# Windowed attention and expert routing on one Trainium2 core: the filling transposes get a PSUM bank of their own, the routing constants become one product, scales are spread in bfloat16

## The chip, the cores and the metric

One NeuronCore of a Trainium2 chip runs the whole kernel; the other cores are idle. The metric is the device time of one execution in microseconds (us). TensorE (PE) multiplies matrices out of SBUF into PSUM, VectorE (DVE) and ScalarE (ACT) work element by element, GpSimd (POOL) does so too and issues the gathers and scatters, SyncE (SP) issues most DMAs.

## The reference, cut to what matters

Four batches of eight heads, 768 positions and 64 dimensions go through a windowed attention; its output is 3072 tokens of 512 values, which a mixture of eight experts works on. Every expert takes exactly 384 tokens, and which ones is settled greedily over all 3072 x 8 scores:

```
logits = x @ w_gate
order = np.argsort(-logits.flatten())
for idx in order:
    tok, e = idx // E, idx % E
    if assigned[tok] >= 0 or counts[e] >= cap: continue     # cap = 384
    assigned[tok] = e; counts[e] += 1
...
for e in range(E):
    h = np.maximum(x[assigned == e] @ w1[e], 0.0)           # 384 x 512 x 1024
    out[assigned == e] = h @ w2[e]                          # 384 x 1024 x 512
```

## The kernel before, in words

**Attention** (lines 55 to 266) runs over 24 tiles of 128 tokens as a software pipeline: scores (L104), softmax on DVE and ACT (L112 to L116), transposes (L123, L192), the product with the values (L138), logits (L203, L213). SP loads each tile's keys, values and queries into one of five buffers (L92) when the buffer is free. POOL and ACT build a two-part float16 copy of each token row (L172 to L174), and SP stores it to memory (`xs`, L182).

**Constants** (L917 to L963) are made while the attention runs: one table is loaded into `cc`, and POOL casts its pieces (L935, L948), after which DVE copies some of them into a PSUM tile `R` (L952 to L958). `constants` is a generator that is advanced once per attention tile; all nine casts and `pairs` stand in one step of it.

**Routing** (`phase`, L461) finds one expert's 384 tokens at a time. For each of the first seven experts it makes four rounds of a search: DVE builds two masks (L384), PE counts into a histogram `ps` (L396), DVE clips it (`hs`, L510), PE forms running counts (L522, L524), DVE counts the cells at or over 384 (`rc`, L529), PE spreads the result over all partitions (L533 with a base, L534 with the counts), and DVE takes the maximum (`nm`, L537). After the fourth round the expert's number is known (`ei`, L544; the weight loads of that expert wait for it), and slots follow: a scan (L569), the offset of each partition (L579, L580), masks (L594 to L601), a product that sorts the token numbers (L631, L636), the numbers themselves (`ids`, L642), and three gathers of token rows by POOL (L647). For the first expert POOL first clears a row of the three targets (L627), after a small read `seen` that waits for all stores of `xs` (L625).

**Experts**: each expert's weights come as float32 tiles of 128 x 1024 (L736, 16 buffers). ACT takes their absolute sums (L749), PE and DVE make a power of two of them (L752, L754, L758, `pow2`), PE spreads it over the partitions (L761, with a float32 row of ones), ACT copies it (L766) and scales and rounds the weights (L788, L790), POOL makes the low parts (L799, L816). For the first expert the rows are transposed on PE (`turn`, L674) and copied by ACT and DVE (L677, L679). `gemm` does 96 products of 128 x 384 (L862) and 72 of 128 x 512 (L877) per expert, three passes each for high and low parts. The loads of the first expert's second matrix are held back by a one-element ACT copy (L731).

**What sets the order.** `Lines` (L406) is a planner. Every line of work is a generator that names an engine, an estimated cost and a ready time; `run` takes the line that can start first and emits its instructions, so these estimates set each engine's program order. While the first expert is being routed nothing else is there for PE, so `fill` (L454) puts dummy transposes of a 128 x 128 identity matrix into the planned gaps. Before, they write into columns 384 to 448 of the PSUM tile `D`:

```
n = int((t - self.clk[PE] - 0.2) / 0.11)
for _ in range(n):
    g.nc.tensor.transpose(g.D[:, 384:448].bitcast(F16), g.ident16, g.ident16)
```

`D` is one bank, and it also holds the histogram, the running counts, the offsets, `quads` and a row of ones, each of which DVE or ACT reads or writes.

Of the kernel before, what the change touches and what calls it, by code (L numbers as in the profile page):

```python
# [11 lines left out]
F32 = mybir.dt.float32  # L12
F16 = mybir.dt.float16
BF16 = mybir.dt.bfloat16
# [5 lines left out]
P = 128  # L20
# [4 lines left out]
NT = N // P  # L25
# [376 lines left out]
LATE, SEM = 0.25, 0.1  # L402
# [3 lines left out]
class Lines:  # L406
# [47 lines left out]
    def fill(self, t):  # L454
        g = self.g
        n = int((t - self.clk[PE] - 0.2) / 0.11)
        for _ in range(n):
            g.nc.tensor.transpose(g.D[:, 384:448].bitcast(F16), g.ident16, g.ident16)  # L458


def phase(g, k, out):  # L461
# [12 lines left out]
    if k < E - 1:  # L474
# [11 lines left out]
        for r in range(4):  # L486
            if k or r:
# [5 lines left out]
                for a, b in zip(cuts, cuts[1:]):  # L493
# [8 lines left out]
                    p = yield PE, 0.2 + 0.015 * (b - a), max(e + SEM, p)  # L502
# [24 lines left out]
            rc = t([64, 1], F16, "rc")  # L527
# [7 lines left out]
            e = yield DVE, 0.55, p + LATE  # L535
# [20 lines left out]
    e = yield DVE, 1.6, e  # L556
# [12 lines left out]
    v.tensor_tensor_scan(R.sc, g.one48, gq.rearrange("p a n -> p (a n)"), 0.0, op0=ALU.mult, op1=ALU.add)  # L569
# [3 lines left out]
    v.tensor_scalar(g16, gq, 1.0 / 16, None, op0=ALU.mult)  # L573
# [3 lines left out]
    p = yield PE, 0.3, e + SEM  # L577
# [39 lines left out]
def tokens(g, k, out, lo, hi, e):  # L617
# [10 lines left out]
    p = yield PE, 0.45, e + SEM, soon  # L628
# [85 lines left out]
def loads(g, k, st):  # L714
# [25 lines left out]
def weights(g, k, st, n):  # L740
# [20 lines left out]
    nc.tensor.matmul(g.D[:, 106:108], g.one_row, pr.rearrange("p a b -> p (a b)"), start=True, stop=True)  # L761
# [155 lines left out]
def constants(g, consts):  # L917
# [9 lines left out]
    for t, x in ((g.ones, 1.0), (g.one_row, 1.0), (g.esum, 28.0)):  # L927
        nc.gpsimd.memset(t, x)
    for _ in range(5):
        yield  # L930
    g.e8 = c["e8"]

    def cast(n, dt, rows=P):
        t = g.fixed.tile([rows, c[n].shape[1]], dt, name="c_" + n)
        nc.gpsimd.tensor_copy(t, c[n][:rows])  # L935
        return t

    g.upper = cast("upper", BF16)
    g.tri2, g.eye2 = (cast(n, F16).rearrange("p (a m) -> p a m", a=2) for n in ("tri2", "eye2"))
    g.blk, g.base = cast("blk", F16, 64), cast("base", BF16, 2)  # L940
# [7 lines left out]
    nc.gpsimd.tensor_copy(pairs, c["io"][:, 0:E * 8].unsqueeze(2).to_broadcast([P, E * 8, 2]))  # L948
# [4 lines left out]
    nc.vector.memset(R.z0, 0.0)  # L953
    nc.vector.tensor_copy(R.idc.bitcast(I32), idc.bitcast(I32))
    g.one48 = g.D[:, 204:252]
    nc.vector.memset(g.one48, 1.0)
    nc.vector.memset(g.one48[:, NT:NT + 1], 0.0)
    nc.vector.tensor_copy(R.e8, g.e8)  # L958
    g.quads = g.D[:, 448:480].bitcast(BF16).rearrange("p (n t) -> p n t", t=4)
    quads = g.fixed.tile([P, 16, 4], BF16, name="quads")  # L960
    nc.gpsimd.tensor_copy(quads, c["six"].unsqueeze(2).to_broadcast([P, 16, 4]))
    g.quads0 = quads
    yield  # L963
# [3 lines left out]
def attention_moe(ctx: ExitStack, tc: tile.TileContext, kv, w_gate, w1, w2, consts, out):  # L967
# [14 lines left out]
    g.ones = g.fixed.tile([P, P], BF16, name="ones")  # L982
    g.one_row = g.fixed.tile([1, P], F32, name="one_row")
# [6 lines left out]
    with tc.manual_schedule():  # L990
        with (tc.tile_pool(name="abuf", bufs=1) as g.abuf, tc.tile_pool(name="kvbuf", bufs=1) as g.kvbuf,
# [9 lines left out]
            g.lines, g.cold, g.open = Lines(g), INF, False  # L1001
# [13 lines left out]
        g.wbuf = ctx.enter_context(tc.tile_pool(name="wbuf", bufs=1))  # L1015
        g.lines.run()
# [23 lines left out]
CONST_COLS = [("io", P), ("e8", E), ("tri2", 2 * 64), ("eye2", 2 * 64), ("blk", E), ("base", E), ("upper", P),  # L1040
# [3 lines left out]
def const_table():  # L1044
# [9 lines left out]
    c["blk"] = 1024 * ((a // 8 == np.arange(E)[None, :]) & (a < 64))  # L1054
# [64 lines left out]
```

## Time and profile before

| what | value |
|---|---|
| three runs, median (lowest to highest) | 450.91 us (448.26 to 451.80) |
| the profiled execution's own time | 450.91 us |
| its span, first to last instruction | 448.9 us |
| mean granted TensorE clock | 0.968 of 2.4 GHz |
| DVE, ACT, POOL busy | 291.6, 312.6, 256.2 us |

The span is read in three stages: attention up to about 105 us, the routing of the first expert up to about 147 us, and the experts after that, in which the routing of the next expert runs between the products of the current one. An engine's idle time is costly only where the chain that ends last goes through it. In the rows below, L12 is line 12 of the kernel before, and `D`, `R` and so on are its tiles.

### The profile page before, as it was taken

What the parts mean: (1) busy time and instruction counts of PE and PEld (TensorE: products, weight loads), DVE (VectorE), ACT (ScalarE), POOL (GpSimd) and SP (SyncE); (2) the same over time, 40 slices, a digit from 0 to 9 for tenths busy, and PEclk for the clock granted to TensorE, in tenths of its full rate; (3) what the DMA queues carried; (4) which work ended last, traced back from release to release, by engine and by line L of the source; (5) the groups of instructions that cost most, each with busy time, mean ns of one, the idle gap of its engine ahead of it and who ended that gap; (6) DMA issues with size and microseconds to landing.
All of it is one profiled execution on the core that took longest, in us unless ns stands there. A gap on an engine that the chain in (4) does not pass through costs nothing.

```text
span 448.9 us, 10820 instructions
## 1 busy us (share of the span) xinstructions
PE 400.8 (89%) x4097; PEld 245.1 (55%) x4097; DVE 291.6 (65%) x1087; ACT 312.6 (70%) x518; POOL 256.2 (57%) x220
## 2 busy tenths in 40 slices
PE   1889889995766997999999999999999999999993
PEld 1767677773655553465456445545545645545541
DVE  5476767976666668778868867967976872322210
ACT  6387786884114776978958868887796779996500
POOL 6065765651535838755657395477277538957501
PEclk9999999998858899999999999999999999999999
DMA  7898898957853507907913942960881586961001
GB/s 226 363 396 291 305 342 301 331 215 214 164 171 111 189 1 275 286 26 262 267 59 105 366 95 66 364 159 23 302 239 48 163 294 176 329 165 47 1 23 47
DMA packets 43059, 87.61 MB, mean 195 GB/s; under 512 B 25216, under 2 KB 25344, under 8 KB 40064
## 3 DMA queue, kind: packets, MB, share of 16 engines
q1 hardware_dynamic: 38848, 73.88, 50.5%
q0 software_dynamic: 3872, 12.60, 8.5%
q8 instruction: 32, 0.52, 0.5%
q10 hardware_dynamic: 288, 0.45, 0.3%
q14 instruction: 19, 0.16, 0.1%
HBM read 68.82 MB, written 12.60 MB: 181 GB/s over the span
## 4 chain that ended last, share of the span: by engine, by line
PE 62%; DVE 16%; DMA 9%; issue 7%; POOL 3%; ACT 2%; SPq 0%; POOLq 0%; DVEq 0%; ACTq 0%
PE ps_y L877 22%; PE ps_hid L862 19%; DMA kvb<-in_kv_dram 6%; PE ps_av L138 3%; PE D L458 3%; PE ps_s L104 3%; PE D L396 2%; DVE g L573 2%; PE ps_pt L123 2%; DVE hl L829 1%; DMA w1f<-in_w_dram 1%; PE ps_xt L192 1%; PE D L203 1%; PE D L522 1%; PE D L761 1%
## 5 line engine op out<-in xcount | busy, mean ns | idle before, releaser
L862 PE MATMUL ps_hid<-x,w1h 128*128 128x384 f16 x512 | 100.9, 330 | 0.2 <-DVE hl L829 0.2
L799 POOL TENSOR_TENSOR w2l<-w2f,w2h 128x1024 f16<-128x1024 f32 x32 | 67.9, 2132 | 24.1 <-ACT w2h L790 24.0
L799 POOL TENSOR_TENSOR w1l<-w1f,w1h 128x1024 f16<-128x1024 f32 (+1 forms) x33 | 67.9, 2072 | 13.6 <-ACT w1h L790 12.8
L862 PEld LDWEIGHTS <-w1h 128*128 128x128 f16 x512 | 47.8, 98 | 30.0 <-issue 1.3
L877 PEld LDWEIGHTS <-hh 128*128 128x128 f16 x384 | 35.1, 98 | 39.7 <-issue 2.2
L862 PE MATMUL ps_hid<-x,w1l 128*128 128x384 f16 x256 | 54.1, 326 | 0.0
L829 DVE SCALAR_TENSOR_TENSOR hl<-ps_hid,hh 128x384 f16<-128x384 f32 x64 | 35.3, 552 | 26.7 <-ACT hh L826 26.5
L749 ACT ACTIVATE jk<-w1f 128x1024 f16<-128x1024 f32 x32 | 33.8, 1056 | 24.0 <-DMA w1f<-in_w_dram 23.3
L877 PE MATMUL ps_y<-w2l,hh 128*128 128x512 f16 x192 | 49.4, 380 | 0.0
L877 PE MATMUL ps_y<-w2h,hh 128*128 128x512 f16 x192 | 47.7, 379 | 1.8 <-ACT hh L826 1.0
L647 POOL DMA_INDIRECT xg<-xs,ids x24 | 23.1, 962 | 44.8 <-DVE R L329 8.7
L877 PE MATMUL ps_y<-w2h,hl 128*128 128x512 f16 x192 | 47.0, 379 | 0.0
L826 ACT ACTIVATE hh<-ps_hid 128x384 f16<-128x384 f32 x64 | 30.9, 483 | 22.8 <-PE ps_hid L862 22.6
L172 POOL TENSOR_TENSOR xr<-x,sxp 128x512 f32<-128x512 f32 x24 | 24.9, 1039 | 36.2 <-DVE sxp L708 21.9
L885 POOL DMA_INDIRECT out_dram<-y,ids x24 | 23.9, 995 | 32.2 <-DVE y L837 24.6
L174 POOL TENSOR_TENSOR keep<-xr,keep 128x512 f16<-128x512 f32 x24 | 27.0, 1127 | 24.6 <-ACT keep L173 24.3
L104 PE MATMUL ps_s<-kvb 128*32 128x128 f32 x768 | 28.9, 291 | 13.5 <-DMA kvb<-in_kv_dram 13.4
L837 DVE TENSOR_SCALAR y<-ps_y,inv,xg 128x512 f32<-128x512 f32 x24 | 19.3, 805 | 28.3 <-PE ps_y L877 27.6
L788 ACT ACTIVATE w1f<-w1f,s1s 128x1024 f32<-128x1024 f32 (+1 forms) x31 | 34.4, 1110 | 0.5
L788 ACT ACTIVATE w2f<-w2f,s2s 128x1024 f32<-128x1024 f32 x30 | 34.2, 1140 | 0.5
L749 ACT ACTIVATE jk<-w2f 128x1024 f16<-128x1024 f32 x32 | 33.7, 1053 | 0.9
L790 ACT ACTIVATE w1h<-w1f 128x1024 f16<-128x1024 f32 (+1 forms) x31 | 31.9, 1029 | 1.3
(193 smaller groups left out, 762.2 us busy)
## 6 DMA issues: line engine op xcount, KB each, us to landing
kvb<-in_kv_dram SPq DMA_DIRECT2D x46, 580.0 KB, 6.2
w1f<-in_w_dram SPq DMA_DIRECT2D x32, 512.0 KB, 6.0
w2f<-in_w_dram SPq DMA_DIRECT2D x32, 512.0 KB, 8.5
xs<-keep SPq DMA_DIRECT2D x24, 256.5 KB, 5.0
kvb<-in_kv_dram SPq DMA_DIRECT2D x2, 320.0 KB, 3.3
kvb<-in_kv_dram SPq DMA_DIRECT2D x2, 260.0 KB, 4.3
xg<-xs,ids POOLq DMA_INDIRECT x24, 3.8
out_dram<-y,ids POOLq DMA_INDIRECT x24, 2.8
```

The costliest lines, as they stand in the source:

```text
L104: nc.tensor.matmul(o, s["q"][:, pr, c, :], s["k"][:, :, 2 * pr + c // 2, 0:2 + c % 2:1 + c % 2], start=True, stop=True, tile_position=(0, ...
L172: nc.gpsimd.tensor_tensor(xr, s["x"], sx[:, 0].to_broadcast([P, DM]), op=ALU.mult)
L174: nc.gpsimd.tensor_tensor(row[:, DM:2 * DM], xr, row[:, 0:DM], op=ALU.subtract)
L749: nc.scalar.activation(jk, fl[j][0], AF.Abs, accum_out=am[:, j:j + 1])
L788: nc.scalar.activation(fc, fc, AF.Copy, scale=s[:, 0:1])
L790: nc.scalar.activation(hc, fc, AF.Copy)
L799: g.nc.gpsimd.tensor_tensor(l, f, h, op=ALU.subtract)
L826: g.nc.scalar.activation(hh[:, f], ph[:, 0:CAP], AF.Relu)
L829: g.nc.vector.scalar_tensor_tensor(hl[:, f], ph[:, 0:CAP], 0.0, hh[:, f], op0=ALU.max, op1=ALU.subtract)
L862: nc.tensor.matmul(ph[:, 0:CAP], w[:, f // 2, kc, (f % 2) * P:(f % 2) * P + P], st[x][:, kc, :], start=(n == 0), stop=(n == 3 * KC - 1))
L877: nc.tensor.matmul(py, h[:, f, c], w[:, f, :], start=(n == 0), stop=(n == 3 * FC - 1))
L885: sc = g.nc.gpsimd.indirect_dma_start(out=g.out, in_=y, in_offset=None, out_offset=bass.IndirectOffsetOnAxis(ap=ids, axis=0))
```

## The change

The change has these parts.

1. **A bank for filling transposes.** `fill` writes to a tile `fill` in bank C of the second PSUM pool. It counts on 0.125 us for one instead of 0.11 and leaves 0.3 us free instead of 0.2. The pool exists only once the attention's pool is closed, which the planner reaches after the second round, so no fills are made before; and none after the third gathered tile is to be transposed, when the bank is given back. There are 98 fills instead of 179.
2. **The count and the base in one product.** The constant `blk` gets two rows for the base, `rc` gets two rows of ones, and L533 and L534 become one matmul per round.
3. **Scales spread by their upper halves.** The scale is a power of two, so its upper 16 bits are its bfloat16 value; L761 reads these, and the row of ones is bfloat16.
4. **Constants two a tile**: after every second cast the generator yields, and it begins two tiles earlier; DVE's copies are spread in the same way.
5. The scan (L569) multiplies by a constant of `R` instead of one of `D`; the offsets take a product with `lower` (L580); L573 becomes an operation with one operand in PSUM.
6. Estimates: `ROOM` = 0.2 in place of `SEM` = 0.1 for PE's steps of later experts, and other costs; the hold of the second matrix's loads waits, in the plan, for the first expert's rows to be ready.

```
-        n = int((t - self.clk[PE] - 0.2) / 0.11)
+        n = int((t - self.clk[PE] - 0.3) / 0.125) if g.filler is not None else 0
         for _ in range(n):
-            g.nc.tensor.transpose(g.D[:, 384:448].bitcast(F16), g.ident16, g.ident16)
+            g.nc.tensor.transpose(g.filler, g.ident16, g.ident16)
...
-            v.tensor_scalar(jk, cum, float(CAP), 0.0, op0=ALU.is_ge, op1=ALU.add, accum_out=rc)
+            v.tensor_scalar(jk, cum, float(CAP), 0.0, op0=ALU.is_ge, op1=ALU.add, accum_out=g.rc[0:64])
-            nr = 1 if r < 3 else 2
-            nc.tensor.matmul(ne, g.ones[0:nr], g.base[0:nr], start=True, stop=False)
-            nc.tensor.matmul(ne, rc.to_broadcast([64, P]), g.blk, start=False, stop=True)
+            n = 65 if r < 3 else 66
+            nc.tensor.matmul(ne, g.rc[0:n].to_broadcast([n, P]), g.blk[0:n], start=True, stop=True)
...
-    v.tensor_tensor_scan(R.sc, g.one48, gq.rearrange("p a n -> p (a n)"), 0.0, ...)
+    v.tensor_tensor_scan(R.sc, R.e8[:, 1:2].to_broadcast([P, 2 * NT]), gq.rearrange("p a n -> p (a n)"), 0.0, ...)
-    v.tensor_scalar(g16, gq, 1.0 / 16, None, op0=ALU.mult)
+    v.scalar_tensor_tensor(g16..., gq..., 1.0 / 16, R.e8[:, 1:2].to_broadcast([P, 2 * NT]), op0=ALU.mult, op1=ALU.mult)
-    nc.tensor.matmul(off, g.ones, g.rz[:, 0:2], start=False, stop=True)
+    nc.tensor.matmul(off, g.lower, g.rz[:, 0:2], start=False, stop=True)
...
+    if a == NG - 1:                                   # in turn(), the third tile
+        g.filler = None
+        g.lines.bank["C"].append(0.0)
...
-                yield ACT, 0.2, lambda: src[m - 1][0] if len(src) >= m else INF, 5.0
+                yield ACT, 0.2, (lambda: src[m - 1][0] if len(src) >= m else INF) if k else lambda: st.get("x", INF), 5.0
...
-    nc.tensor.matmul(g.D[:, 106:108], g.one_row, pr.rearrange("p a b -> p (a b)"), start=True, stop=True)
+    halves = pr.rearrange("p a b -> p (a b)").bitcast(BF16).rearrange("p (a t) -> p a t", t=2)
+    nc.tensor.matmul(g.D[:, 106:108], g.one_row, halves[:, :, 1], start=True, stop=True)
...
+    for i, (a, b) in enumerate(made):                 # in constants()
+        nc.gpsimd.tensor_copy(a, b)
+        if i % 2:
+            yield
...
+        g.filler = g.lines.take("C", [P, P], "fill", F16)
```

The order on the engines follows. On PE, in the first expert's second round, this stood between the running counts (`c_tri`) and the spreading of the result, with the semaphore waits in brackets (the first fill waits for DVE):

```order
423 L524 MATMUL D<-hs,c_tri_708 64x32
424 L458 LDWEIGHTS ident_64
425 L458 MATMUL D<-ident_64 128x128 [waits DVE_49]
426 L458 LDWEIGHTS ident_64
427 L458 MATMUL D<-ident_64 128x128
```

Six such pairs stood there, and behind them, before the next fills, the two products of `c_base` and `rc`. In the changed kernel the first two rounds have no fills. In its last round two stand at this place, without a wait, and the one product that is left waits for DVE itself:

```order
379 L524 MATMUL D<-hs,c_tri_538 64x32
380 L458 LDWEIGHTS ident_64
381 L458 MATMUL fill<-ident_64 128x128
382 L458 LDWEIGHTS ident_64
383 L458 MATMUL fill<-ident_64 128x128
384 L532 LDWEIGHTS rc [waits DVE_49]
385 L532 MATMUL D<-c_blk,rc 128x8
386 L458 LDWEIGHTS ident_64
```

The fills lost their wait, and the wait moved to the product that needs the count. On ACT, where the first expert's weights (`w1h`) and rows (`x`) are made ready, the hold of the second matrix (`w2f`, L731) stood ahead of the three copies of the rows:

```order
150 L766 ACTIVATE s1s<-D 128x2
151 L788 ACTIVATE w1f<-w1f,s1s 128x4x128
152 L790 ACTIVATE w1h<-w1f 128x4x128
153 L731 ACTIVATE w2f<-xg 1x1
154 L677 ACTIVATE x_2539<-ps_xg 128x4x128 x3
155 L788 ACTIVATE w1f<-w1f,s1s 128x4x128
```

and now stands behind them:

```order
150 L768 ACTIVATE s1s<-D 128x2
151 L790 ACTIVATE w1f<-w1f,s1s 128x4x128
152 L792 ACTIVATE w1h<-w1f 128x4x128
153 L678 ACTIVATE x_2461<-ps_xg 128x4x128 x3
154 L732 ACTIVATE w2f<-xg 1x1
155 L790 ACTIVATE w1f<-w1f,s1s 128x4x128
```

So these loads start three copies later against the rows. On POOL, among the row work of the attention (L172, L174), the constants stood in one run:

```order
30 L935 CAST c_upper<-cc 128x128
31 L935 CAST c_tri_708<-cc 128x128
32 L935 CAST c_eye_710<-cc 128x128
33 L935 CAST c_blk<-cc 64x8
34 L935 CAST c_base<-cc 2x8
35 L935 CAST c_shift<-cc 128x8
36 L935 CAST c_mask<-cc 128x8
37 L943 MEMSET rz 128x3
38 L935 CAST c_idc<-cc 128x48
39 L935 CAST c_put<-cc 128x128
40 L948 CAST pairs<-cc 128x128
```

and now two stand between the rows of one tile and of the next:

```order
27 L957 CAST c_upper<-cc 128x128
28 L957 CAST c_lower<-cc 128x128
29 L172 TENSOR_TENSOR xr<-x,sxp 128x512
30 L174 TENSOR_TENSOR keep<-xr,keep 128x512
31 L957 CAST c_tri_538<-cc 128x128
32 L957 CAST c_eye_539<-cc 128x128
```

So the run of eleven is cut into pairs with a tile's row work between them; DVE's copy of `pairs` into `R` (L952) is now emitted two tiles after POOL's cast of it, instead of directly behind it.

## Rows read from the trace of the kernel before

**Rows 1.** The page's busy times of PE and its weight loads, with the engines behind them, over the whole span (busy us, share of the span, instructions).
```profile
PE 400.8 (89%) x4097; PEld 245.1 (55%) x4097; DVE 291.6 (65%) x1087; ACT 312.6 (70%) x518; POOL 256.2 (57%) x220
```

**Rows 2.** Busy time by stretch, from the answer on ten stretches of the span: start and end, length, busy us (and instructions) of PE, weight loads, DVE, ACT, POOL, then the granted clock, the DMA share and GB/s.
```profile
105.00:147.00 42.00, 27.76 (x320) 23.73 (x321) 27.19 (x128) 13.05 (x38) 16.89 (x16) 0.71 0.61 161
...
378.00:411.00 33.00, 33.00 (x180) 17.38 (x178) 9.13 (x25) 28.84 (x44) 26.40 (x20) 1.00 0.60 191
```

**Rows 3.** The chain that ended last, between 98 and 152 us: start, length, what. The four rounds of the first expert's search, where the chain goes through the fills (L458).
```profile
111.10 0.80 PE D L458 x6
...
112.51 0.91 PE D L458 x7
113.41 0.11 PE D L533
...
116.61 0.33 PE D L458 x3
...
117.45 0.49 PE D L458 x6
...
120.91 0.33 PE D L458 x3
...
121.74 0.49 PE D L458 x6
...
125.35 0.48 PE D L458 x3
...
126.44 0.48 PE D L458 x3
```

**Rows 4.** The timeline of the slots of the first expert: start, length, engine, instruction, count, and in brackets the idle time before with what ended it.
```profile
129.03 0.16 DVE L570 TENSOR_SCALAR rz<-R 128x2 bf16<-128x2 f32 x1
129.04 2.29 PE L458 MATMUL D<-ident 128*128 128x128 f16 x20 [1.89 <-DVE R L569]
...
131.41 0.25 DVE L584 SCALAR_TENSOR_TENSOR R<-gq,D,R 128x24 f32<-128x24 f32 x1 [1.42 <-PE D L580]
...
132.92 3.14 PE L458 MATMUL D<-ident 128*128 128x128 f16 x28 [1.55 <-DVE one L594]
...
133.38 0.45 DVE L601 TENSOR_TENSOR hi<-su,R 128x576 bf16<-128x576 bf16 x1
...
135.86 0.68 PE L631 MATMUL D<-hi,lo 128*128 128x96 bf16 x6
...
136.89 0.33 PE L458 MATMUL D<-ident 128*128 128x128 f16 x3 [0.35 <-DVE own L634]
```

**Rows 5.** The same timeline, from the expert number to the first expert's first product: POOL's clears and gathers, SP's weight loads, the scale, the first rounded weights, the rows' copies and the hold.
```profile
127.44 2.77 POOL L627 MEMSET xg<- 1x1026 f16 x3
...
128.58 1.98 SPq L736 DMA_DIRECT2D w1f<-in_w_dram  x4
...
137.14 1.06 ACT L749 ACTIVATE jk<-w1f 128x1024 f16<-128x1024 f32 x1 [0.30 <-DMA w1f<-in_w_dram]
...
138.73 1.04 POOL L647 DMA_INDIRECT xg<-xs,ids  x1 [8.53 <-DVE k_x L331]
...
140.90 0.14 DVE L752 TENSOR_REDUCE am<-am 128x1 f32<-128x4 f32 x1
...
142.74 0.17 ACT L766 ACTIVATE s1s<-D 128x2 f32<-128x2 f32 x1 [4.45 <-PE D L761]
...
143.70 0.63 ACT L790 ACTIVATE w1h<-w1f 128x512 f16<-128x512 f32 x1
...
145.17 0.20 ACT L731 ACTIVATE w2f<-xg 1x1 f32<-1x1 f16 x1 [0.83 <-DMA xg<-xs,ids]
...
145.28 1.52 ACT L677 ACTIVATE x<-ps_xg 128x512 f16<-128x512 f16 x3
...
147.32 1.47 PE L862 MATMUL ps_hid<-x,w1h 128*128 128x384 f16 x4
```

**Rows 6.** The chain between 170 and 192 us, the spreading of a scale in a later expert.
```profile
181.87 0.31 PE D L761 x2
```

**Rows 7.** Groups of PE's instructions from 147 us to the end: line, operation, shapes, count, busy us and mean ns of one, idle before.
```profile
L533 PE MATMUL D<-c_base,ones 1*128 1x8 bf16 (+1 forms) x24 | 4.2, 174 | 0.0
...
L761 PE MATMUL D<-s2p,one_row 1*128 1x2 f32 x16 | 3.0, 256 | 0.4 <-DVE s2p L710 0.4
...
L761 PE MATMUL D<-s1p,one_row 1*128 1x2 f32 x14 | 2.6, 256 | 0.0
```

**Rows 8.** Who PE waited for from 147 us to the end: us in total, times, longest.
```profile
PE D L631 <- DVE hi L601: 2.1, 4, 0.8
```

**Rows 9.** The chain between 40 and 82 us, at the constants: POOL's first cast, and DVE's next piece of the attention after the copies.
```profile
45.27 0.23 POOL c_upper L935
...
47.99 0.67 DVE mx L112
```

**Rows 10.** Busy time, granted clock and DMA share in short stretches, columns as in rows 2.
```profile
52.00:56.00 4.00, 4.00 (x120) 3.63 (x116) 2.58 (x9) 3.22 (x8) 2.50 (x3) 1.00 0.74 232
...
114.00:116.00 2.00, 2.00 (x25) 2.00 (x25) 1.93 (x8) 0.00 (x0) 0.00 (x0) 0.50 1.10 213
...
144.00:146.00 2.00, 1.53 (x16) 1.29 (x14) 1.01 (x3) 1.17 (x4) 2.00 (x3) 0.50 0.18 72
...
152.00:154.00 2.00, 2.00 (x24) 1.28 (x22) 1.56 (x5) 2.00 (x3) 1.39 (x2) 1.00 0.40 156
```

More of the change, by code (lines that the diff above doesn't have):

```diff
@@ L401 @@
 NONE, PE, DVE, ACT, POOL, DMA, TURN = "", "PE", "DVE", "ACT", "POOL", "DMA", "TURN"
-LATE, SEM = 0.25, 0.1
+LATE, SEM, ROOM = 0.25, 0.1, 0.2
 HALF = 1.5 * BIG
@@ L555, in phase @@
     gq, gt = t([P, 2, NT], F32, "gq"), t([P, NT], F32, "gt")
-    e = yield DVE, 1.6, e
+    e = yield DVE, 1.4, e
     if k < E - 1:
@@ L627, in tokens @@
             nc.gpsimd.memset(x[0:1], 0.0)
-    p = yield PE, 0.45, e + SEM, soon
+    p = yield PE, 0.45 if k < 1 else 0.3, e + (ROOM if k else SEM), soon
     pair = g.D[:, 108:204]
@@ L926, in constants @@
         o += wd
-    for t, x in ((g.ones, 1.0), (g.one_row, 1.0), (g.esum, 28.0)):
+    for t, x in ((g.one_row, 1.0), (g.esum, 28.0)):
         nc.gpsimd.memset(t, x)
-    for _ in range(5):
+    for _ in range(3):
         yield
     g.e8 = c["e8"]
+    made = []
     def cast(n, dt, rows=P):
         t = g.fixed.tile([rows, c[n].shape[1]], dt, name="c_" + n)
-        nc.gpsimd.tensor_copy(t, c[n][:rows])
+        made.append((t, c[n][:rows]))
         return t
-    g.upper = cast("upper", BF16)
+    g.upper, g.lower = cast("upper", BF16), cast("lower", BF16)
     g.tri2, g.eye2 = (cast(n, F16).rearrange("p (a m) -> p a m", a=2) for n in ("tri2", "eye2"))
-    g.blk, g.base = cast("blk", F16, 64), cast("base", BF16, 2)
+    g.blk = cast("blk", BF16, 66)
+    g.rc = g.fixed.tile([66, 1], BF16, name="rc")
+    nc.gpsimd.memset(g.rc, 1.0)
     g.shift, g.mask = cast("shift", I32), cast("mask", I32)
@@ L947, in constants @@
     pairs = g.fixed.tile([P, E * 8, 2], BF16, name="pairs")
-    nc.gpsimd.tensor_copy(pairs, c["io"][:, 0:E * 8].unsqueeze(2).to_broadcast([P, E * 8, 2]))
+    made.append((pairs, c["io"][:, 0:E * 8].unsqueeze(2).to_broadcast([P, E * 8, 2])))
+    quads = g.quads0 = g.fixed.tile([P, 16, 4], BF16, name="quads")
+    made.append((quads, c["six"].unsqueeze(2).to_broadcast([P, 16, 4])))
+    for i, (a, b) in enumerate(made):
+        nc.gpsimd.tensor_copy(a, b)
+        if i % 2:
+            yield
     yield
@@ L953, in constants @@
     nc.vector.memset(R.z0, 0.0)
+    yield
     nc.vector.tensor_copy(R.idc.bitcast(I32), idc.bitcast(I32))
-    g.one48 = g.D[:, 204:252]
-    nc.vector.memset(g.one48, 1.0)
-    nc.vector.memset(g.one48[:, NT:NT + 1], 0.0)
+    yield
     nc.vector.tensor_copy(R.e8, g.e8)
     g.quads = g.D[:, 448:480].bitcast(BF16).rearrange("p (n t) -> p n t", t=4)
[L960 to L963, printed above, removed]
 @with_exitstack
@@ L1000, in attention_moe @@
                 next(att)
-            g.lines, g.cold, g.open = Lines(g), INF, False
+            g.lines, g.cold, g.open, g.filler = Lines(g), INF, False, None
             experts(g, st)
@@ L1037, in tile @@
         return pool.tile(shape, dt, tag=tag, name=name, bufs=n)
-CONST_COLS = [("io", P), ("e8", E), ("tri2", 2 * 64), ("eye2", 2 * 64), ("blk", E), ("base", E), ("upper", P),
+CONST_COLS = [("io", P), ("e8", E), ("tri2", 2 * 64), ("eye2", 2 * 64), ("blk", E), ("upper", P), ("lower", P),
                ("idc", 2 * NT), ("put", P), ("own", 4), ("row", 8), ("shift", 8), ("mask", 8), ("six", 16)]
@@ L1053, in const_table @@
     c["eye2"] = (half & (r == b)[:, None, :]).reshape(P, 128)
-    c["blk"] = 1024 * ((a // 8 == np.arange(E)[None, :]) & (a < 64))
-    c["base"] = np.where(a == 0, BIG, np.where(a == 1, np.arange(E)[None, :], 0))
+    c["blk"] = np.where(a < 64, 1024 * (a // 8 == np.arange(E)[None, :]), np.where(a == 64, BIG, np.where(a == 65, np.arange(E)[None, :], 0)))
+    c["lower"] = a > p[None, :]
     c["upper"] = a < p[None, :]
```

13 lines of the change are left out of this document (6 added, 7 removed).

## The prediction

> **What bounds the kernel now.** I read the page's busy times first: PE 89% of the span, more than any other engine [rows 1]. A share over the whole span hides where PE is held up, so I took busy time by stretch next. In the stretch of 33 us late in the experts PE is busy for all of it; in the 42 us of the first expert's routing it is busy for 27.76 at a mean clock of 0.71, and DVE for 27.19, so neither is full [rows 2]. There the chain alternates between DVE and PE, and each piece stands in series. The chain of waits then shows something odd: several of its pieces are the filling transposes, L458, which compute nothing [rows 3]. The timeline says why. A fill stands in PE's program ahead of a product that is needed, and it begins only when DVE has finished reading some part of D: the bracket behind a run of 20 names the scan L569, the one behind 28 names L594 [rows 4]. So a gap that should have been filled while DVE worked is filled after it, and the product and DVE wait for the end of the fills. The fills are on the path; the experts behind are bound by PE's own instructions.
>
> **The sum**, against the profiled execution: 450.91 us, which is also the median of the three runs, with a span of 448.9 and 2.0 around it.
>
> *Rounds of the first expert.* In round one the fills on the chain took 0.80 and 0.91, in rounds two and three 0.33 and 0.49, in round four 0.48 and 0.48; the extra product L533 took 0.11 in each [rows 3]. Rounds one and two lose their fills: 0.80 + 0.91 + 0.33 + 0.49 = 2.53. Rounds three and four keep one to four at these places, but none that waits for DVE, and each run fits into the gap in which DVE makes the clipped histogram or the count: 0.33 + 0.49 + 0.48 + 0.48 = 1.78. Four products L533 are 0.44. Sum 4.75. Without fills PE may spend rounds two and three at the lower level; seven fills took 0.91 there and six 0.49 at the higher, so a few small matmuls cost some 0.15 more in the two rounds. I take 4.6; the ends are 2.5 (only the dropped fills) and 5.2.
>
> *Slots of the first expert.* The offsets' input is ready at 129.03 + 0.16 = 129.19, but DVE gets the offsets at 131.41, since 20 fills begin at 129.04 [rows 4]. In a bank of their own the 17 that are left begin when PE falls idle, 1.89 earlier at 127.15, and at 2.29 / 20 = 0.115 each end at 129.1. Two products at 0.17 [rows 7] then give DVE its offsets at about 129.6: 1.8 won. At L594 PE was idle 1.55 before 28 fills; 25 at 3.14 / 28 = 0.112 begin at 131.37 and end at 134.2, after the last mask (133.38 + 0.45 = 133.83), so the sort begins at 134.2 instead of 135.86: 1.7. The three fills of 0.33 behind `own` go as well: 0.3. Sum 3.8; the ends are 0 (the fills still wait) and 4.1.
>
> The token numbers so come 4.6 + 3.8 = 8.4 earlier. *Who is late next?* POOL's clears end at 127.44 + 2.77 = 130.21; the first gather would move from 138.73 to 130.3, so even clears that don't move at all are just in time. The weight loads hang on the expert number and move by the rounds' 4.6: the last sum ends at 138.20 - 4.6 = 133.6. DVE took it up only at 140.90, because the next expert's keys stood ahead, and these move by 8.4; so the sum is taken up at 133.6. From there to the scale's end (142.74 + 0.17) were 2.0, and 1.4 more to the first rounded weights (143.70 + 0.63): 137.0. The rows are ready at 145.28 + 1.52 - 8.4 = 138.4 [rows 5]. The rows are still last, by 1.4, and the first product moves from 147.32 to 138.9. The six fills and the histogram that stood ahead of it ran while ACT copied the rows; the histogram now comes after one product and costs what the fills gave back, so I count nothing there.
>
> *The hold.* L731 came at 145.17, ahead of copies that end at 146.80 [rows 5]; the second matrix's loads now start some 1.6 later against the rows. Their cover is the first matrix's 96 products: four took 1.47 at the lower level, so 0.18 each at the higher, 17 us in all. I take 0; if that cover is too short, up to 1.6 is lost.
>
> *Later experts.* 24 products L533 are left out [rows 7]; at the 0.11 of the chain [rows 3], 2.6. The scale's spreading stands 30 times as two float32 passes, that is 15 pairs [rows 7]; a pair is 0.31 on the chain [rows 6], and one bfloat16 pass should be like the small product's 0.11: 0.20 x 15 = 3.0. No row shows the single pass of this shape. Sum 5.6, since PE is full there; the ends are 0, if another engine is late, and 24 x 0.174 + 15 x 0.256 = 8.0 by the whole durations.
>
> *Waits in PE's queue.* The largest is for the last mask, 2.1 us in four waits [rows 8]. The shorter L573 and the planner's wider margin should shrink it, and the re-planned order can make others; I take 0, with 2.1 to either side.
>
> *Constants.* The chain runs from POOL's first cast at 45.27 through all of them and DVE's copies to DVE's next piece of the attention at 47.99 [rows 9], 2.7 us as the upper end. But the attention also lives on its loads: behind that stall the DMA share fell to 0.74 over 4 us [rows 10], which is 1.0 us of transfers not done. A kernel bound by loads gains these, and I take 1.0; the lower end is 0. One cast more, `lower`, stands beside POOL's waits.
>
> Sum: 4.6 + 3.8 + 5.6 + 1.0 = 15.0, so 450.9 - 15.0 = 435.9 us.
>
> **Rivals.** *The clock.* Before, PE was at a granted clock of 0.50 (1.2 GHz, the lower of its two levels) in 114 to 116, at 0.50 again in 144 to 146, and back at 1.00 in 152 to 154, some 5 us after the first product [rows 10]. The change has 98 fills instead of 179 and none in two rounds; if PE's clock therefore rises later, each us of products at the lower level costs half a us. With 10 us more it is 5.0: 440.9. Against it: the runs of 17, 25 and 28 fills lie closer together than before, as they don't wait. The Trainium skill (TensorE: Matmul & The Clock Gate, section Part 1: The HAM clock gate) says that the slow state is the default and that activity lifts it, which speaks against dropping fills; the rows named above agree that the level falls in the thin stretch and returns under dense products, and no row tells how few fills are too few.
>
> *The experts don't follow.* If weights or loads are late where PE gets faster, the 5.6 are not seen: 441.5. For it: the other engines move with the same planner. Against it: PE is busy 33.00 of 33.00 in the late stretch while ACT has 28.84 and POOL 26.40 [rows 2].
>
> *The bank frees nothing.* If the fills are still ordered behind DVE, the 3.8 and the 1.78 of rounds three and four go: 435.9 + 5.6 = 441.5. The order shows the fills without a wait, so this is unlikely.
>
> *Slower.* The merged product L533 needs the count itself, so it waits where L533 could run ahead before, and behind it in PE's queue stand the products of the current expert, for which ACT and DVE wait. The longest wait of such a small product now is 0.8 [rows 8]. If each of the 24 later rounds stalled PE that long, 19.2 would be lost: 435.9 + 19.2 = 455.1. It decides from 15.0 / 24 = 0.63 per round.
>
> **How the numbers follow.** Forecast 0.72, clock 0.12, experts 0.10, bank 0.03, slower 0.03. The likeliest gives 435.9. Its upper ends (constants 1.7, experts 2.4, waits 2.1 more) reach 429.7; the rivals on the faster side end at 441 to 441.5, and 1.6 for the hold on top gives 443. So 430 to 443 leaves out the slower case, the clock's tail and some of the forecast's own. A measurement of this kernel can tell about 1%, 4.5 us, from no change. Slower by more is the last rival, 0.03; within 1% I put a long clock tail (over 20 us at the lower level) and half-failed sums, 0.05; faster by more has the rest, 0.92.
>
> **What would show it.** Right: fills without a bracket that names DVE; offsets back at DVE within 0.5 of its scan's end; the first L862 between 138 and 139 less the constants' 1.0; the scale's spreading once per scale at about 0.11 on the chain; no stall at POOL's casts. Wrong: a first product after 141; a granted clock at 0.50 more than 5 us into the products; PE waits from 147 on that sum to clearly more than before, above all behind the merged product; weights instead of rows released last before the first product.

## The result and the profile after

The changed kernel takes 431.44 us, the median of four runs (431.13 to 431.98), beside 451.08 for the kernel before (448.26 to 451.80): a ratio of 0.958, 95% interval 0.954 to 0.962. The prediction was 435.9 within 430 to 443; the time is 4.5 below it, near the range's lower end. The profiled execution has a span of 429.5, so 19.4 less than before, where 15.0 were forecast.

Four marks cut the span: the end of the attention (L214 copies the last logits), the reduction that makes the token numbers (`ids`, L640), the first product (L864) and the end. They are read off each timeline as start times, here for all kernels in the order in which the runs are discussed:

| kernel | attention end | to `ids` | `ids` to first product | first product to end | ratio of the times to before (95%) |
|---|---|---|---|---|---|
| before | 106.74 | 30.85 | 9.73 | 301.6 | 1 |
| after | 105.89 | 23.24 | 9.20 | 291.2 | 0.958 (0.954, 0.962) |
| bank_alone (on before) | 106.87 | 23.84 | 10.19 | 303.6 | 0.989 (0.985, 0.994) |
| before_no_fills | 106.93 | 23.75 | 10.92 | 300.8 | 0.984 (0.977, 0.991) |
| fills_in_d (on after) | 108.11 | 26.40 | 8.86 | 293.0 | 0.962 (0.955, 0.968) |
| no_fills | 104.99 | 23.39 | 8.83 | 291.4 | 0.961 (0.955, 0.966) |
| two_counts | 108.27 | 23.78 | 11.51 | 296.0 | 0.975 (0.970, 0.980) |
| f32_spread | 102.58 | 23.42 | 11.14 | 294.1 | 0.968 (0.963, 0.974) |
| room_as_before | 104.82 | 23.26 | 12.89 | 293.1 | 0.967 (0.962, 0.972) |
| g16_as_before | 108.99 | 23.22 | 13.49 | 290.8 | 0.965 (0.959, 0.971) |
| consts_one_step | 108.00 | 23.24 | 10.47 | 291.6 | 0.960 (0.952, 0.968) |
| hold_as_before | 105.78 | 23.27 | 10.70 | 293.6 | 0.957 (0.951, 0.964) |
| more_fills | 110.98 | 23.26 | 10.76 | 291.9 | 0.958 (0.954, 0.962) |
| more_fills_turn | 105.54 | 23.25 | 11.90 | 292.8 | 0.964 (0.959, 0.970) |

The profiled executions of g16_as_before and more_fills were slow ones, 1.5% or more above the fastest of their kernels, and their first and third columns (108.99 and 13.49, 110.98 and 10.76) are left out of the ranges that follow. The columns are not equally firm. The attention's end lies anywhere from 102.6 to 108.3 for the same work, and `ids` to first product from 8.8 to 12.9, which fits the spread of 1% and more among the times of one kernel; the way to `ids` is 23.22 to 23.42 in all eight kernels with the same order of work there. The last but one column reads 291.2 to 293.0 in four kernels with the same instructions there (after, no_fills, fills_in_d, consts_one_step), a scatter of some 2. So small effects are read from these columns and from the rows, not from the ratios.

PE's busy time fell from 400.8 to 384.1 us, at the same share of 89% [rows 1].

The timeline of the slots in the changed kernel answers [rows 4] (start, length, engine, instruction, count, in brackets the idle time before and what ended it):

```profile
122.24 1.98 PE L458 MATMUL fill<-ident 128*128 128x128 f16 x17
...
124.25 0.16 DVE L568 TENSOR_SCALAR rz<-R 128x2 bf16<-128x2 f32 x1
...
124.47 0.16 PE L577 MATMUL D<-rz,c_upper 128*128 128x2 bf16 x1 [0.26 <-DVE rz L568]
...
124.52 2.83 PE L458 MATMUL fill<-ident 128*128 128x128 f16 x25
...
125.31 0.25 DVE L582 SCALAR_TENSOR_TENSOR R<-gq,D,R 128x24 f32<-128x24 f32 x1
...
127.27 0.45 DVE L599 TENSOR_TENSOR hi<-su,R 128x576 bf16<-128x576 bf16 x1
...
127.77 0.42 PE L629 MATMUL D<-hi,lo 128*128 128x96 bf16 x6 [0.42 <-DVE hi L599]
```

No fill names DVE any more. The 17 fills of 1.98 end before `rz`; the offsets' products begin 0.06 after `rz` ends (124.25 + 0.16), and DVE takes the offsets at 125.31 behind its own pieces, where [rows 4] have 2.2 between the two. The 25 fills end before the last mask `hi` (127.27 + 0.45), and the sort waits for this mask alone.

The same timeline up to the first product answers [rows 5]:

```profile
129.13 0.25 DVE L640 TENSOR_REDUCE ids<-idf 128x3 int32<-128x96 f32 x1
...
133.39 0.16 DVE L753 TENSOR_REDUCE am<-am 128x1 f32<-128x4 f32 x1 [0.87 <-ACT jk L750]
...
133.60 0.27 PE L755 MATMUL D<-ident,am 128*1 128x128 f32 x1 [3.23 <-DVE am L753]
...
134.83 0.16 PE L763 MATMUL D<-s1p,one_row 1*128 1x2 bf16 x1 [0.62 <-DVE s1p L711]
...
135.36 2.72 PE L675 MATMUL ps_xg<-ident,xg 128*128 128x128 f16 x24 [0.37 <-issue]
...
136.52 1.77 ACT L678 ACTIVATE x<-ps_xg 128x512 f16<-128x512 f16 x3
...
138.33 0.48 PE L864 MATMUL ps_hid<-x,w1h 128*128 128x384 f16 x1 [0.26 <-ACT x L678]
```

Here the step "rows last" fails: PE idled 3.23 until the weights' sum (`am`), and the 24 transposes of the rows stand behind the scale's spreading (L763) in its program. From the end of `am` (133.55) it takes 4.8 to the first product. The weights are last, not the rows. In this execution it is close: the last gather lands at 136.66 (145.08 before, so the 8.4 that were forecast), and PE reaches its rows at 137.02, 0.4 later. (The histogram that stood ahead of the first product before, 0.64 on the chain here, now follows it, so some 0.6 changes sides between the last two columns.)

The clock, in stretches with the columns of [rows 10]:

```profile
136.00:138.00 2.00, 2.00 (x20) 1.91 (x18) 1.50 (x4) 1.90 (x4) 2.00 (x2) 0.50 0.04 12
...
140.00:142.00 2.00, 2.00 (x14) 0.96 (x13) 0.33 (x3) 1.73 (x2) 1.40 (x3) 0.75 0.93 338
142.00:144.00 2.00, 2.00 (x15) 1.21 (x13) 1.97 (x7) 1.43 (x2) 2.00 (x2) 1.00 1.04 389
...
158.00:161.50 3.50, 2.37 (x15) 0.93 (x14) 2.83 (x18) 3.42 (x5) 3.50 (x3) 1.00 0.15 22
161.50:165.00 3.50, 3.50 (x9) 1.24 (x9) 3.18 (x14) 1.08 (x2) 3.50 (x3) 0.52 0.97 353
```

The granted clock is 0.50 when the products start and back at 1.00 by 142, within 3.7 us of the first product, where [rows 10] allow nearly 5: it does not rise later than before, as the clock rival had it. But the prediction's sign of being wrong, a granted clock at 0.50 more than 5 us into the products, did come: from 161.5 to 165, 23 us in, behind 3.5 us in which PE was busy for 2.37. At half speed for 3.4 us that costs at most 1.7. Seven of the 14 profiled executions have such a stretch, 22 to 47 us behind the first product; no_fills and before_no_fills have none, so it is not for want of fills.

In the experts the chain and PE's groups answer [rows 6 to 8] (chain: start, length, what; groups: count, busy us, mean ns, idle before):

```profile
146.91 0.01 PE D L532
...
154.10 0.12 PE D L763
```

```profile
L532 PE MATMUL D<-c_blk,rc 65*128 65x8 bf16 (+1 forms) x24 | 4.1, 172 | 0.0
...
L629 PE MATMUL D<-hi,lo 128*128 128x96 bf16 x42 | 2.9, 204 | 0.0
...
L763 PE MATMUL D<-s2p,one_row 1*128 1x2 bf16 x8 | 1.3, 169 | 1.2 <-DVE s2p L711 1.2
```

The spreading takes 0.12 on the chain instead of 0.31, as forecast. The merged product takes 0.01, where the two it replaces took 0.11 each. The waits for the masks and for `own` (2.1 and 1.2 before) are 0.0 and 0.1; those for a scale's sums and for `s2p` are 1.3 and 1.2 (0.2 and 0.4 before). All listed waits of PE from the first product on sum to 5.5 instead of 6.7.

### The profile page after: what moved, and what is told of

Its sections match the earlier page's. It is cut to its first block, busy times and chain, and to the rows that moved or that the text cites. A ratio compares the mean times of both kernels' runs of the same rounds, so it can differ in the third digit from the quotient of the medians.

```text
span 429.5 us, 10568 instructions
## 1 busy us (share of the span) xinstructions
PE 384.1 (89%) x3972; PEld 233.9 (54%) x3972; DVE 283.5 (66%) x1085; ACT 311.7 (73%) x518; POOL 256.1 (60%) x220
## 4 chain that ended last, share of the span: by engine, by line
PE 63%; DMA 12%; DVE 8%; issue 6%; ACT 5%; POOL 3%; SPq 2%; POOLq 0%; DVEq 0%; ACTq 0%
PE ps_hid L864 23%; PE ps_y L879 23%; DMA kvb<-in_kv_dram 6%; PE ps_av L138 4%; PE ps_s L104 3%; DMA w1f<-in_w_dram 3%; PE ps_pt L123 2%; PE D L396 2%; PE ps_xt L192 1%; PE D L203 1%; ACT w2f L790 1%; DMA xg<-xs,ids 1%; ACT w2h L792 1%; POOL w2l L801 1%; SPq L657 1%
## 5 line engine op out<-in xcount | busy, mean ns | idle before, releaser
L864 PE MATMUL ps_hid<-x,w1h 128*128 128x384 f16 x512 | 98.3, 328 | 0.8 <-DMA x<-xg 0.5
L801 POOL TENSOR_TENSOR w2l<-w2f,w2h 128x1024 f16<-128x1024 f32 x32 | 67.9, 2132 | 18.4 <-ACT w2h L792 18.3
L801 POOL TENSOR_TENSOR w1l<-w1f,w1h 128x1024 f16<-128x1024 f32 (+1 forms) x33 | 67.7, 2072 | 10.5 <-ACT w1h L792 10.2
L864 PEld LDWEIGHTS <-w1h 128*128 128x128 f16 x512 | 47.8, 98 | 31.6 <-issue 1.7
L864 PE MATMUL ps_hid<-x,w1l 128*128 128x384 f16 x256 | 54.6, 326 | 0.0
L879 PE MATMUL ps_y<-w2h,hl 128*128 128x512 f16 x192 | 48.1, 387 | 0.0
L172 POOL TENSOR_TENSOR xr<-x,sxp 128x512 f32<-128x512 f32 x24 | 25.0, 1040 | 33.3 <-DVE sxp L709 21.3
L174 POOL TENSOR_TENSOR keep<-xr,keep 128x512 f16<-128x512 f32 x24 | 27.1, 1127 | 24.3 <-ACT keep L173 24.1
L839 DVE TENSOR_SCALAR y<-ps_y,inv,xg 128x512 f32<-128x512 f32 x24 | 19.4, 807 | 28.7 <-PE ps_y L879 27.6
```

The source lines that it names most:

```text
L172: nc.gpsimd.tensor_tensor(xr, s["x"], sx[:, 0].to_broadcast([P, DM]), op=ALU.mult)
L174: nc.gpsimd.tensor_tensor(row[:, DM:2 * DM], xr, row[:, 0:DM], op=ALU.subtract)
L801: g.nc.gpsimd.tensor_tensor(l, f, h, op=ALU.subtract)
L864: nc.tensor.matmul(ph[:, 0:CAP], w[:, f // 2, kc, (f % 2) * P:(f % 2) * P + P], st[x][:, kc, :], start=(n == 0), stop=(n == 3 * KC - 1))
L879: nc.tensor.matmul(py, h[:, f, c], w[:, f, :], start=(n == 0), stop=(n == 3 * FC - 1))
```

## The experiments

### What the fills cost: four kernels

fills_in_d puts the changed kernel's fills back into D:

```
-        g.filler = g.lines.take("C", [P, P], "fill", F16)
+        g.lines.take("C", [P, P], "fill", F16)
+        g.filler = g.D[:, 384:448].bitcast(F16)
```

> The changed kernel, its filling transposes written to 64 columns of D again instead of a bank of their own; same number of fills, same program order on every engine. Bank theory (a fill in D is ordered behind every DVE read of D that stands ahead of it in the program): the scan no longer reads D, so the 17 fills ahead of the offsets stay free (+0.1 at most); the 25 fills ahead of the sort start only when DVE has read quads out of D (126.76 instead of 124.52) and end at about 129.6, so the sort starts 1.8 later, the first product moves from 138.33 to about 140.2 and the time from 431.4 to about 433.3. The prediction's sum (both runs of fills wait): +3.5, 434.9. Count rival (only the number of fills mattered): 0, 431.4.

PE's timeline of this kernel (its whole clock runs 2.2 later, by the attention's end):

```profile
120.90 0.58 PE L458 MATMUL D<-ident 128*128 128x128 f16 x4 [0.28 <-DVE jk L528]
...
125.89 1.97 PE L458 MATMUL D<-ident 128*128 128x128 f16 x17 [0.26 <-DVE nm L535]
...
130.08 2.83 PE L458 MATMUL D<-ident 128*128 128x128 f16 x25 [2.16 <-DVE one L592]
```

Every run now names DVE, and the way to `ids` is 26.40 instead of 23.24: 3.2 lost. I had expected 1.8 from the sort's run alone; the fills between the running counts and the merged product (0.58 and 0.37) go on the chain as well, and the runs behind the rounds start only after `nm`. The prediction's 3.5 is nearer. The count rival (0) is out.

no_fills leaves `g.filler` at None:

> The changed kernel with no filling transposes at all (98 fewer instructions pairs on PE), otherwise the same order. Theory that the fills now lie wholly beside DVE's work: nothing to win, the ids come at about 129.4 as with fills, PE's small products run at 1.2 GHz in 126 to 134 too (+0.3 to +0.6), and the clock returns about as late as with the fills (it is at 0.50 in 136 to 140 with them as well): +0.5, about 431.9. Clock rival: without the fills the clock rises some 4 us later into the products, +2 or more: 433.5 to 436.

```profile
132.00:136.00 4.00, 2.37 (x20) 1.90 (x20) 3.25 (x14) 2.17 (x6) 2.86 (x3) 0.50 0.53 161
136.00:138.00 2.00, 1.74 (x20) 1.41 (x20) 1.36 (x5) 1.80 (x5) 2.00 (x2) 0.50 0.00 0
...
140.00:142.00 2.00, 2.00 (x16) 1.21 (x14) 1.74 (x6) 1.92 (x3) 1.34 (x2) 1.00 1.03 395
```

The way to `ids` is 23.39, inside the 23.22 to 23.42 of the kernels with fills, and the rest as long as with them (291.4). The clock is 0.50 all the way up to the products and 1.00 by 140, 2.8 us after the first product at 137.21. So the 98 fills of the changed kernel cost nothing and buy nothing: the full clock that they raise (1.00 in 128 to 132) is gone before the products start.

bank_alone and before_no_fills are made from the kernel before, the one with the fills in a tile of bank C (as in part 1 of the change, with the old numbers), the other with

```
-        n = int((t - self.clk[PE] - 0.2) / 0.11)
+        n = 0
```

> The kernel before, with the bank for the fills alone (same 179 fills, their count and the planner's numbers as before; no fills once that bank is given back to the last row transposes, and none while the attention still runs). Bank theory: the runs of 20 and 28 fills no longer wait for DVE (1.8 + 1.7) and those on the chain in the rounds begin when PE falls idle; with the rounds' 4.3 us of fills half hidden the first product moves from 147.3 to about 141.7 and the time from 451 to about 445.4 (3.5 to 8 us less). Count rival: the bank frees nothing, 0 to 1 us less, 450 to 451.

> The kernel before with no filling transposes at all. If the fills on its chain were pure loss: rounds 4.3 and slots 3.5 to 3.8 less, minus some 0.5 because the small products run at 1.2 GHz: about 443.5, first product near 140. If the fills held up the clock at the products: the clock comes back later than 5 us after the first product and half of the gain is lost: 446 or more. If the fills lie in gaps anyway: 451.

The bank alone takes 7.0 off the way to `ids` (30.85 to 23.84), and leaving out all fills takes 7.1: in D the fills were a loss of 7 us, in their own bank they lie wholly in the gaps. bank_alone is not quite the bank alone: it makes 121 fills and not the 179 that its expectation names, since the bank is not there yet in the first two rounds (52 fewer) and is given back before the first product (6 fewer). That fills in D wait, and what that costs at one and the same number of fills, is shown by fills_in_d. The whole change takes 7.6, so the fewer fills, the merged product and the other scan add 0.6 here. On the whole time the bank alone is 1.1% and no fills 1.6%.

### The products that were merged and shortened

two_counts has two products in a round again, with their constants:

```
-            n = 65 if r < 3 else 66
-            nc.tensor.matmul(ne, g.rc[0:n].to_broadcast([n, P]), g.blk[0:n], start=True, stop=True)
+            nr = 1 if r < 3 else 2
+            nc.tensor.matmul(ne, g.ones[0:nr], g.base[0:nr], start=True, stop=False)
+            nc.tensor.matmul(ne, g.rc[0:64].to_broadcast([64, P]), g.blk[0:64], start=False, stop=True)
...
```

> The changed kernel with the merged count product taken apart again into two (a base product that waits for nothing, then the count's), with its ones and base constants back. Theory from the two traces: a small product alone hides its weight load behind the product ahead, two in a row show one load and about 0.1 of a second product, so 0.2 per round in 24 rounds plus 0.11 in four: +5.2, 436.6. The prediction's own number: 0.11 per round, +3.0, 434.4. Rival that the merging gave nothing and the gain came from fewer waits: 0, 431.4.

The experts take 296.0 instead of 291.2, and the way to `ids` 0.5 more. That is 4.8 / 24 = 0.2 per round, nearer to my expectation than to the prediction's 0.11. But my reason for it, that a small product alone hides its weight load, is wrong, as two timelines of PE and its weight loads (PEld) show. First two_counts, then the changed kernel around a scale's product and a merged one:

```profile
186.50 0.48 PE L865 MATMUL ps_hid<-x,w1h 128*128 128x384 f16 x2 [0.18 <-DMA x<-xg]
...
186.91 0.09 PEld L532 LDWEIGHTS <-ones 1*128 1x128 bf16 x1 [0.32 <-issue]
186.91 0.17 PE L532 MATMUL D<-c_base,ones 1*128 1x8 bf16 x1
187.02 0.09 PEld L533 LDWEIGHTS <-rc 64*128 64x128 bf16 x1
187.02 0.18 PE L533 MATMUL D<-c_blk,rc 64*128 64x8 bf16 x1
...
187.13 0.66 PE L865 MATMUL ps_hid<-x,w1h 128*128 128x384 f16 x3
```

```profile
186.01 0.98 PE L864 MATMUL ps_hid<-x,w1h 128*128 128x384 f16 x5
...
186.91 0.09 PEld L763 LDWEIGHTS <-one_row 1*128 1x128 bf16 x1 [0.32 <-issue]
186.92 0.17 PE L763 MATMUL D<-s2p,one_row 1*128 1x2 bf16 x1
...
187.02 0.34 PE L864 MATMUL ps_hid<-x,w1h 128*128 128x384 f16 x1
187.03 0.10 PEld L532 LDWEIGHTS <-rc 65*128 65x128 bf16 x1
187.20 0.17 PE L532 MATMUL D<-c_blk,rc 65*128 65x8 bf16 x1
...
187.23 0.48 PE L864 MATMUL ps_hid<-x,w1h 128*128 128x384 f16 x2
```

The scale's product (`one_row`, 1 row) stands alone, and its load still starts only with the product itself, as do those of `ones` (1 row) and of the 64 rows of `rc` in two_counts: each pushes the next product back by 0.10 to 0.11. The load of the 65 rows of `rc` starts at 187.03 beside a product that began at 187.02, and the next large product begins 0.03 after the merged one. The late load costs twice, since it also waits for most of the product ahead: the last product of 384 columns begins at 186.66 in both timelines, its successor would follow 0.16 later, and the small load begins only at 186.91. From the start of the large product ahead to the start of the next one (0.16 or 0.22 us with nothing between), the pair adds 0.31 to 0.32 in 22 of its 23 places between large products in two_counts, the merged product 0.03 to 0.04 in 22 of 23: 0.28 a round, or 6.7 in 24. The 4.8 of the column differ from that by no more than its scatter. A scale's single row adds 0.20.

It is the form of the load that decides here, and the change got 65 rows by the way. The number of rows is not all of it: the loads of `c_eye`, 128 rows but 64 columns, also begin only 0.25 or 0.31 after the start of the large product ahead. The Trainium skill (TensorE: Matmul & The Clock Gate, section Architectural detail: the array is 16× 32×32, not 1× 128×128) says that PE's queue can pull weight loads ahead of products in flight; the trace agrees for 65 and 128 rows and not for 1 and 64. Why, is open; a scale spread with padded rows wasn't tried.

f32_spread puts the float32 row back:

```
-    nc.tensor.matmul(g.D[:, 106:108], g.one_row, halves[:, :, 1], start=True, stop=True)
+    nc.tensor.matmul(g.D[:, 106:108], g.one_row, pr.rearrange("p a b -> p (a b)"), start=True, stop=True)
...
```

> The changed kernel with the scale spread as a float32 row again (two passes) instead of the upper halves in bfloat16. Prediction's number: 0.31 against 0.11 on the chain, 15 scales: +3.0, 434.4. Rival, by whole durations (0.256 against 0.170): +1.3, 432.7. Rival that these lie in waits: 0.

The experts take 294.1, 2.9 more, and each scale on the chain is as before:

```profile
184.75 0.31 PE D L762 x2
```

That fits 0.20 x 15 = 3.0 and not 1.3. The column alone, with its scatter of 2, could not tell these apart; the rows do: between large products the two passes add 0.40 where the single one adds 0.20, in 12 of 14 places each.

### The planner's margin and DVE's shorter piece

room_as_before sets `ROOM = 0.1`; g16_as_before makes L571 a float32 `tensor_scalar` again.

> The changed kernel with the planner's margin ahead of PE lines that wait for DVE put back from 0.2 to 0.1 (later experts' histograms, offsets and sort stand earlier in PE's order). Theory: the waits for the last mask and the sort come back in part, which were 3.3 us in all before and 0.1 after: +1 to +2, 432.4 to 433.4. Rival: the shorter DVE piece alone removed them, 0: 431.4.

> The changed kernel with the sixteenth of the masks made by the float32 tensor_scalar form again instead of scalar_tensor_tensor (same order on all engines). It took 0.18 us alone but a median of 1.43 and up to 2.07 us before, where POOL worked beside it. Theory: DVE's chain to the sort is over 1 us longer in seven experts and the PE waits for masks come back, +1 to +2: 432.4 to 433.4. Rival: it lies beside PE's products, 0: 431.4.

With the old margin the experts take 293.1, 1.9 more, or 2.5 with the 0.64 of a histogram that stands ahead of its first product again, and PE's waits from the first product on sum to 10.0 instead of 5.5. But these are not the waits that were expected back; the largest are for scales' sums and low parts (us in total, times, longest):

```profile
PE D L755 <- DVE am L753: 2.4, 3, 1.1
PE ps_hid L864 <- DVE hl L831: 1.8, 2, 1.5
```

These waits are longer than in any other variant, but 293.1 lies at the edge of the column's scatter (291.2 to 293.0), so what the margin is worth in time is not shown. With the old form of L571 the waits for masks do come back:

```profile
L571 DVE TENSOR_SCALAR g<-gq x8: 177/313/2004, 127.4 to 352.4; 128x48 f32<-128x48 f32 x8
```

```profile
PE D L629 <- DVE hi L599: 1.1, 3, 0.8
PE D L634 <- DVE own L632: 0.9, 1, 0.9
```

```profile
307.06 2.13 POOL L801 TENSOR_TENSOR w2l<-w2f,w2h 128x1024 f16<-128x1024 f32 x1 [0.61 <-ACT w2h L792]
...
307.23 2.00 DVE L571 TENSOR_SCALAR g<-gq 128x48 f32<-128x48 f32 x1
```

It takes 0.18 to 2.0 us where the new form took 0.19 to 0.20 in all eight places. Yet the experts take 290.8: 2.0 of waits returned and no time. What makes up for them no run shows; it lies within that column's scatter. Each of the four slow cases (0.45 to 2.0) begins while POOL subtracts low parts (L801, 2.1 us) and ends 0.04 after that instruction, as the last two rows show (309.19 and 309.23). The Trainium skill (SBUF — State Buffer, section Who interferes with whom) says that GpSimd and some forms on VectorE lock each other out for a whole instruction, which these ends agree with; no run here takes POOL's work away.

### Constants and hold

consts_one_step makes all casts in one step again; hold_as_before takes the change out of `loads`.

> The changed kernel with all casts of the constants in one step of the attention again (and DVE's copies behind them in one step). The prediction's number: a stall of POOL and DVE of up to 2.7 us stands on the chain again at the sixth or seventh tile, and the attention ends 1.0 later: 432.4. Rival: the attention lives on its loads and takes the stall back from its buffers: the stall is seen on the chain, the end of the attention does not move by it. The attention's end has lain anywhere between 102.6 and 109 in the executions profiled so far, so the time alone cannot tell 1 us; the chain around the casts has to.

```profile
44.90 0.21 POOL c_upper L957
...
47.69 0.60 DVE mx L112
```

The chain goes through all casts and copies again, 2.9 us from 44.81 to `mx`; in the changed kernel's chain these microseconds belong to a load and no cast stands on it. What that moves at the attention's end stays open: 108.00 here lies inside the scatter of 102.6 to 108.3.

> The changed kernel with the hold on the second matrix's loads ahead of ACT's row copies again. The prediction's number: these loads' cover (some 17 us of first-matrix products) is enough, so nothing from the first product on (291.2 us to the end), and the loads 0.2 to 1.6 us earlier run beside nothing that is late: 431.4. Rival: the second matrix was late, up to 1.6 less behind the first product, 429.8. Other rival: the earlier loads take bandwidth from the last gather, and the first product comes later against the token numbers (9.2 us) by 0.5 to 1.

The loads start 1.6 before the first product instead of 0.06 behind it, and the experts are no shorter (293.6): the hold costs nothing, as forecast. `ids` to first product (10.70) lies within its scatter, so the last rival isn't decided.

### A try at a better kernel

more_fills emits 60 fills ahead of L755 and 8 ahead of L763 for the first weights; more_fills_turn also lets the row transposes stand ahead of the scale:

```
-    p = yield PE, 1.0, lambda: max(out["at"][a], out.get("s1t", INF)), soon
+    p = yield PE, 1.0, lambda: out["at"][a], soon
```

> The changed kernel with 60 more fills (in their own bank) ahead of the transpose of the first weights' sums and 8 ahead of the scale's spreading, in gaps where PE now idles for 3.2 us and 0.6. Clock theory: PE stays at 2.4 GHz until the products; the 24 row transposes take about 1.7 instead of 2.7 and the first 2.6 us of products are no longer at 1.2 GHz: 1.0 + 1.3 less, 429.1. Rival: the first weights land so late (7 to 9 us after the token numbers in four of the runs, 4.5 in the changed kernel's own profile) that the clock falls again behind the fills: 0, 431.4. Other rival: the fills outlast the wait and delay the scale, +0.4 or more.

> As more_fills, and the planner no longer makes the row transposes wait for the scale: the first 8 of 24 stand between the transpose of the weights' sums and the spreading, the 16 others behind it. Where the weights are last (as in all the runs of the changed kernel so far), 8 transposes leave the path behind the scale: 0.5 to 0.9 less than more_fills, about 428.4. Rival: the gathered rows land later than the weights, and the spreading now waits for them: +0.5 to +1.5 against more_fills.

The clock does stay up:

```profile
142.00:144.00 2.00, 1.50 (x24) 1.43 (x25) 1.97 (x7) 1.94 (x5) 1.85 (x1) 1.00 0.00 0
144.00:146.00 2.00, 1.00 (x17) 0.73 (x16) 1.63 (x8) 1.97 (x5) 2.00 (x3) 1.00 0.01 4
```

The 24 transposes take 1.50 instead of 2.72, and the first ten microseconds behind the first product hold 87 PE instructions instead of 80. Yet neither part of the way gets shorter (10.76 and 291.9), nor the time (0.958 of the kernel before, as for the changed kernel): the first product now waits 1.26 for ACT's copies of the rows, and PE's waits behind it sum to more (8.7, that one included, against 5.5). PE comes to the second matrix 1.2 sooner than in the changed kernel and waits there as long (0.6 and 0.4 in both). What it saved goes into later waits: for the next expert's rows (1.2 against 0.5), a later scale's sum (2.0 against 1.3), `own` (0.6) and a low part (0.4). more_fills_turn is worse, by its own rival: PE reaches the rows before they have landed, and the spreading stands behind them.

```profile
134.92 0.27 PE L758 MATMUL D<-ident,am 128*1 128x128 f32 x1 [0.33 <-DVE am L753]
...
135.58 1.01 PE L675 MATMUL ps_xg<-ident,xg 128*128 128x128 f16 x8 [0.39 <-DMA xg<-xs,ids]
...
137.38 0.18 PE L769 MATMUL D<-s1p,one_row 1*128 1x2 bf16 x1
```

From `am`'s product to the spreading are 2.46 instead of 1.23. Neither beats the changed kernel.

## Why the prediction was right, and by how much each step was off

The span fell by 4.4 more than forecast, and that is the later experts, which gave 4.8 more. Rounds and slots gave 0.8 less; the way from `ids` to the first product gave 0.5, and the attention's end 0.9 for the 1.0 forecast, both inside the scatter of their columns.

*Rounds and slots of the first expert*: 8.4 forecast, 7.6 measured; up to the expert number (`ei`) 3.9 for 4.6, behind it 3.7 for 3.8. Inside the 3.7 two errors cancel: the offsets won 1.3 and not 1.8, as DVE had pieces of its own to do first (its bracket in [rows 4] names 1.42 of idle time, not 2.2), and the sort 2.0 and not 1.7. The mechanism (the fills wait for DVE's reads of D) is shown from both sides, by bank_alone and by fills_in_d. That the fills kept in a bank of their own cost nothing also held.

*Who is late next*: wrong. The rows were to be last by 1.4. In the changed kernel and eight of its ten variants the weights' sum `am` is last and begins 4.7 to 5.3 us ahead of the first product; in fills_in_d the third gather is, and more_fills_turn has another order. `am` itself comes 3.3 (fills_in_d) to 7.6 us (room_as_before) behind `ids`, as the last weight load lands. It cost some 0.4 in the profiled execution, where the first product still came 0.5 earlier against `ids` than before, and more where the loads land later: the first product comes up to 12.9 behind `ids`. That the step did not spoil the sum is luck. The step looked at when the scale is ready and not at the transposes that stand behind it in PE's program.

*Later experts*: 5.6 forecast, 10.4 measured (11 with the histogram that moved into them), the one term that was clearly mis-sized. Scales 3.0, measured 2.9. The merged product 2.6, measured 4.8 by the column and 6.7 by the rows: I took one product off the chain at 0.11, but the pair cost 0.31 a round, and of that 0.03 is left. Waits in PE's queue, which I had at 0 within 2.1, fell by 1.2. By the rows these sum to 3.1 + 6.7 + 1.2 = 11.0, the 11 measured; the stretch at 0.50 behind 161.5 is not in that sum.

*Constants*: the stall left the chain; its worth, 1.0, was not settled (the ends differ by 0.85, inside a scatter of 5.7).

*Rivals*: the clock's is out: dropping all fills left the clock back at 1.00 within 3 us of the first product. The Trainium skill (TensorE: Matmul & The Clock Gate, section Part 1: The HAM clock gate) says that activity lifts the throttle of the clock, and the levels in no_fills and more_fills agree (0.50 and 1.00 ahead of the products); but a level raised ahead of a gap bought nothing. The stretch at 0.50 23 us into the products was on the list of what would show the forecast wrong; it is worth 1.7 at most, and the sum held in spite of it. The experts followed, the bank freed what it should, and the merged product did not stall PE: L532 has no wait of its own in 24 rounds (0.0).

## What to carry to other kernels

A filling instruction is only free if it touches nothing that another engine reads: give it a buffer of its own, and then ask, with a run without fills, whether it buys anything. For a step that becomes earlier, follow the program order of each engine behind it, not only when its inputs are ready. Where a small matrix product stands among large ones, look at when its weight load starts: that, not its own length, is its price.

## What was not expected of the hardware

Weight loads of 1, 2 or 64 rows began only 0.07 us before the end of the product ahead (these ends are the profile's model), and so did those of 64 columns (`c_eye`), while one of 65 rows began beside it: between large products a single row cost 0.20, a row and 64 rows in a pair 0.31, 65 rows 0.03. And the same attention, which lives on loads, ended up to 5.7 us apart in different executions, and 2 MB of weights took from 4.3 to 7.6 us behind the token numbers to be summed, with the same instructions ahead of them.
